# One value block per pair of heads in an attention and mixture-of-experts kernel, with the probabilities of both heads in one tile

## The chip, the core and the metric

The kernel runs on one core of one Trainium2 chip, the other cores idle. The metric is the device time of one execution in microseconds (us). Before the change the median of 3 runs is 830.39 us (829.68 to 831.4).

## What is computed

Causal attention with a bias from accumulated gates for 8 batches of 8 heads, 576 tokens and 64 dimensions per head; then a layer of 8 experts that sends each of the 4608 tokens to one expert and scales its output by the gate. Everything is float32.

```python
scores = scale * np.matmul(q, k.transpose(0, 1, 3, 2))
cum = np.cumsum(np.maximum(s, 0.0), axis=-1)
bias = -(cum[:, :, :, None] - cum[:, :, None, :])
scores = np.where(causal, -1e9, scores + np.minimum(bias, 0.0))
attn = np.exp(scores - np.max(scores, axis=-1, keepdims=True))
attn = attn / (np.sum(attn, axis=-1, keepdims=True) + 1e-09)
x = np.matmul(attn, v)                      # then tokens x 512
e = argmax(x @ w_gate + modality_bias[modality_id])
out = gate * (np.maximum(x @ w1[e], 0.0) @ w2[e])
```

## The kernel before, in words

The first half of the program is attention, the second routing and experts; the change is in the first. Attention goes over 32 **pairs**: one head of two batches (ab = 0, 1) at a time, eight pairs for each of four groups of batches. `run` lays nine steps of each pair out in a row, in the order `ORDER` = 3, 7, 2, 6, 8, 1, 5, 0, 4. Step i below 8 is chunk c = i % 4 of head i // 4: 128 queries against 128(c+1) keys. Step 8 is the last 64 queries of both heads at once, against all 576 keys in two halves of 288.

A **step** is `score`: two matmuls on PE, a high part (L373, KA by QH, called H below) and a low part (L395, KB by QL, called L; for step 8 four of each kind of half length, L408 and L409, h and l), into one of the four PSUM buffers `sp`; a mask and row minimum on DVE (L397, for step 8 L411; R below); an exponential with row sums on ACT (L417, E). Three steps later `trans` follows: PE turns the probabilities 128 by 128 (L427, for step 8 L440; T) into one of two PSUM buffers `pt`, and a copy brings them to the tile PT of the head, on ACT (L430), for step 8 on DVE (four copies, L446).

`tail` runs twice per pair. The **value block** g = 1, for queries 256 to 575, is ten matmuls of the values V by PT (L467), the two heads side by side in halves of the array; it comes two steps after step 8 is turned, when chunks 2 and 3 are in PT as well. Block g = 0, for queries 0 to 255, is four matmuls after the last turn. Each block is copied out of PSUM to oT (ACT L470, and for g = 1 also DVE L474), then multiplied with a small matrix that moves it to tokens by dimensions (`pw`, `pq`, L347, into the one PSUM buffer `ox`; called x below), its row sums are inverted (ACT L479, DVE L480), and DVE multiplies and stores (L489, L491; X below). Every matmul runs as two passes, which the trace shows as two records. `prep` makes the operands of the next pair on POOL (L323, L327), SP moves data with DMAs; `load_v` fetches V of the next pair into one of three buffers.

```python
ORDER = (3, 7, 2, 6, 8, 1, 5, 0, 4)
LAG = 3      # steps from score to trans
TD = 1       # steps from trans to a value block
self.PT = [c.tile([P, PTW], F32, name=f"PT{u}") for u in range(3)]
```

The order in which each engine takes its work comes from a list scheduler that follows the data and the few `issue_after` constraints, so it differs between pairs where other work (routing of a finished group, in the first pairs of the next) lies between. The change reaches `tail`, `trans`, `start`, `score`, `load_v`, `consts` and `run`.

Of the kernel before, what the change touches and what calls it, by code (L numbers as in the profile page):

```python
# [17 lines left out]
P = 128  # L18
KW = 576
# [9 lines left out]
PTDVE = (8,)  # L29
QUIET = (0, 1, 5)  # L30
# [7 lines left out]
class Attn:  # L38
# [3 lines left out]
    def __init__(self, ctx, tc, qkv, s, ident, wg):  # L42
# [14 lines left out]
        self.PT = [c.tile([P, PTW], F32, name=f"PT{u}") for u in range(3)]  # L57
        self.oT = [c.tile([P, 640], F32, name=f"oT{u}") for u in range(2)]
# [10 lines left out]
        sr = t1.tile([P, KW], F32, name="sr")  # L69
# [21 lines left out]
        s8 = t1.tile([P, KW], F32, name="s8")  # L91
# [199 lines left out]
    def consts(self):  # L291
        nc = self.nc
        for u in range(2):
            nc.gpsimd.memset(self.oT[u][:, 512:], 0.0)
        for t in self.PT:
            nc.vector.memset(t[64:, PTW - 64:], 0.0)
# [11 lines left out]
    def load_v(self, pi):  # L308
        V = self.ld.tile([P, 2, 5, 64], F32, name="V", bufs=3)
        self.nc.sync.dma_start(V, self.qkv[pi, :, 4 * KW:].rearrange("p (a j d) -> p a j d", a=2, j=5))  # L310
        return V

# [48 lines left out]
    def start(self, pi, x):  # L361
        st = dict(pi=pi, h=pi % 8, x=x, s={}, high={}, PT=[self.PT[(2 * pi + ab) % 3] for ab in range(2)], V=self.V.pop(pi))
        st["mx"] = self.sm.tile([P, 10], F32, name="mx")
        st["sums"] = self.sm.tile([P, 9], F32, name="sums")
        return st
# [10 lines left out]
    def score(self, st, i):  # L376
# [5 lines left out]
        if i < 8:  # L382
# [4 lines left out]
            t = self.wk.tile([P, 512], F32, name="pe", bufs=6)  # L387
# [31 lines left out]
    def trans(self, st, i):  # L419
        nc = self.nc  # L420
        pe, PT = st["s"].pop(i), st["PT"]
        cp = nc.vector.tensor_copy if i in PTDVE else nc.scalar.copy
        if i < 8:
            ab, c = i // 4, i % 4
            pt = self.ps1.tile([P, 512], F32, name="pt")
            for j in range(c + 1):
                self.pe.append(nc.tensor.transpose(out=pt[:, P * j:P * j + P], in_=pe[:, P * j:P * j + P], identity=self.ident).ins)  # L427
            v = min(P * c, 320)
            w = PT[ab][:, P * c - v:P * c - v + PTS * (c + 1)].rearrange("p (j s) -> p j s", s=PTS)
            cp(w[:, :, v:v + P], pt[:, :P * (c + 1)].rearrange("p (j q) -> p j q", q=P))  # L430
        else:
            for j0, nj in ((0, 4), (4, 1)):
# [8 lines left out]
                for ab in range(2):  # L441
                    if nj == 4:
                        w = PT[ab][:, 128:128 + 4 * PTS].rearrange("p (j s) -> p j s", s=PTS)[:, :, 384:]
                    else:
                        w = PT[ab][:kp, PTW - 64:].unsqueeze(1)
                    cp(w, pt[:kp, :P * nj].rearrange("p (j a q) -> p a j q", a=2, q=64)[:, ab])  # L446

    def tail(self, st, g):
# [3 lines left out]
        for _ in range(TD + g):  # L452
            yield
        q0, q1 = (256, KW) if g else (0, 256)
        o = st["o"] if g else self.ps2.tile([P, 512], F32, name="o")
        oT = self.oT[st["pi"] % 2]

        pe, self.pe = self.pe, []
        nj = 5 if g else 2
        for j in range(nj):  # L460
            f = max(P * j, q0)
            for ab in range(2):
                r = slice(64 * ab, 64 * ab + 64)
                with ExitStack() as after:
                    for i in pe:
                        after.enter_context(self.tc.issue_after(i))
                    m = nc.tensor.matmul(o[r, f - q0:q1 - q0], V[:, ab, j, :], PT[ab][:, PTS * j + f if j < 4 else PTW - 64:PTS * j + q1 if j < 4 else PTW], start=j == 0, stop=j == nj - 1)  # L467
            pe = [m.ins]
        self.wall = m.ins
        nc.scalar.copy(oT[:, q0:q0 + 256], o[:, :256])  # L470
        if g:
            for ab in range(2):
                r = slice(64 * ab, 64 * ab + 64)
                nc.vector.tensor_copy(oT[r, 512 + 64 * ab:576 + 64 * ab], o[r, 256:320])  # L474
        yield
        n = 5 if g else 4
        rs = self.sm.tile([P, 5], F32, name="rs")
        with self.tc.issue_after(self.hold[0]), self.tc.issue_after(self.act):
            nc.scalar.activation(rs[:, :n], st["sums"][:, 4 * g:4 * g + n], AF.Identity, bias=self.eps[:, :1])  # L479
            nc.vector.reciprocal(rs[:, :n], rs[:, :n])  # L480
        xo = self.xo
        for u in range(2):
            c = 2 * g + u
            self.pw_(xo[:, 2 * XW * u:2 * XW * u + 2 * XW], oT[:, P * c:P * c + P], self.pw[:, h, :], start=True, stop=True)
        if g:
            self.pw_(xo[:, 4 * XW:5 * XW], oT[:, 512:], self.pq[:, h, :], start=True, stop=True)
        src = xo[:, :4 * XW].rearrange("p (t d) -> p t d", t=4)
        rv = rs[:, :4].unsqueeze(2).broadcast_to([P, 4, XW])
        nc.vector.tensor_tensor(x[g][:, :, :, h], src.rearrange("p t (d r) -> p t d r", r=2), rv.rearrange("p t (d r) -> p t d r", r=2), ALU.mult)  # L489
        if g:  # L490
            nc.vector.tensor_scalar(x[2][:, 0, :, h], xo[:, 4 * XW:5 * XW].rearrange("p (d r) -> p d r", r=2), rs[:, 4:5], None, ALU.mult)  # L491
# [894 lines left out]
```

## Time and profile before

| | |
|---|---|
| median of 3 runs | 830.39 us |
| profiled execution | 829.02 us, of which the span of recorded instructions is 827.3 us |
| PE busy | 812.1 us (98%) |
| DVE, ACT, POOL busy | 545.6 (66%), 541.3 (65%), 360.5 us (44%) |
| granted TensorE clock, mean | 0.996 of full speed |
| end of attention | about 380 us of the span |

A busy share says how long an engine had some instruction in it, not how fast it went. PE's records overlap (a matmul's record runs on while the next starts), so the distance from one start to the next, in the timeline, tells what a matmul costs; a timeline row gives the start, the time to the end of the last record, the number of records, and in square brackets an idle time and what ended it.

### The profile page before, as it was taken

The numbers are of one execution on the slowest core, as the hardware profiler recorded it, in microseconds if no ns is written. First come the engines' busy times: TensorE is split into PE (matmuls) and PEld (weight loads), VectorE is DVE, ScalarE is ACT, GpSimd is POOL, SyncE is SP. The second block draws the span as 40 slices with busy tenths as digits, with TensorE's granted clock in tenths as the row PEclk, the third lists the DMA queues.
The fourth block names the chain that finished last, engine by engine and source line by source line (L and its number), as shares of the span: only waits on it lengthen the run. The fifth ranks groups of instructions, "written<-read, shape, count | busy, mean of one in ns | idle before, by whom it ended". The sixth has DMA issues, their size and how long they took to land. (4 is left out here: it accounts for less than half of the span.)

```text
span 827.3 us, 16879 instructions
## 1 busy us (share of the span) xinstructions
PE 812.1 (98%) x5692; PEld 695.5 (84%) x5692; DVE 545.6 (66%) x1502; ACT 541.3 (65%) x1292; POOL 360.5 (44%) x384
## 2 busy tenths in 40 slices
PE   7999999999999999999999999999999999999997
PEld 6778877877887878887888899998888999988884
DVE  7666667667666677766489865555666656555874
ACT  6788888888888888885365554444455555444663
POOL 8959768988689867992501000000000000000001
PEclk9999999999999999999999999999999999999999
DMA  7665555866567657738697866655556776555970
GB/s 238 187 195 180 180 179 181 254 223 195 170 182 230 208 155 213 226 97 288 222 381 291 312 259 257 229 202 197 213 201 244 258 258 243 199 202 207 380 247 28
DMA packets 68549, 182.31 MB, mean 220 GB/s; under 512 B 7993, under 2 KB 8889, under 8 KB 68334
## 3 DMA queue, kind: packets, MB, share of 16 engines
q1 hardware_dynamic: 62622, 161.17, 57.5%
q0 software_dynamic: 5840, 20.06, 6.3%
q8 instruction: 45, 0.74, 0.4%
q14 instruction: 42, 0.34, 0.1%
HBM read 144.73 MB, written 26.80 MB: 207 GB/s over the span
## 5 line engine op out<-in xcount | busy, mean ns | idle before, releaser
L1067 POOL DMA_INDIRECT out<-ys,oi x36 | 36.5, 1015 | 368.6 <-ACT ys L1066 297.5
L397 DVE CUSTOM_DVE_ANT_0 pe<-sp,mk 128x512 f32<-128x512 f32 (+3 forms) x256 | 121.2, 487 | 63.2 <-PE sp L395 55.5
L417 ACT ACTIVATE pe<-pe,mx 128x512 f32<-128x512 f32 (+3 forms) x256 | 143.8, 562 | 22.4 <-DVE mx L397 21.0
L427 PE MATMUL pt<-ident,pe 128*128 128x128 f32 x640 | 117.7, 281 | 4.0 <-ACT PT L430 2.8
L430 ACT COPY PT<-pt 128x512 f32<-128x512 f32 (+3 forms) x256 | 106.3, 416 | 13.3 <-PE pt L427 12.6
L1083 ACT ACTIVATE hT<-hp 128x512 fp32r<-128x512 f32 x72 | 42.8, 595 | 93.1 <-PE hp L1081 92.6
L467 PE MATMUL o<-PT,V 128*64 128x320 f32 (+4 forms) x896 | 100.7, 364 | 0.0
L373 PE MATMUL sp<-KA,QH 128*128 128x256 f32 (+2 forms) x256 | 97.3, 389 | 2.5 <-POOL KA L236 2.5
L427 PEld LDWEIGHTS pt<-ident,pe 128*128 128x128 f32 x640 | 75.4, 141 | 26.8 <-ACT PT L430 11.2
L467 PEld LDWEIGHTS o<-PT,V 128*64 128x64 f32 x896 | 58.7, 136 | 41.0 <-issue 9.4
L1081 PE MATMUL hp<-xT,wcb 128*128 128x256 f32 x648 | 89.6, 282 | 0.0
L395 PE MATMUL sp<-KB,QL 76*128 76x256 f32 (+2 forms) x256 | 88.4, 349 | 0.0
L1081 PE MATMUL hp<-xT,wca 128*128 128x256 f32 x624 | 87.3, 282 | 0.5 <-ACT xT L1033 0.5
L327 POOL TENSOR_TENSOR KA<-rawk,KA 64x576 fp32r<-64x576 f32 x62 | 87.0, 1419 | 0.2
L327 POOL TENSOR_TENSOR QL<-rawq,QH 64x576 fp32r<-64x576 f32 x62 | 86.6, 1413 | 0.2
L1084 DVE SCALAR_TENSOR_TENSOR hT<-hp,hT 128x512 fp32r<-128x512 f32 x72 | 49.5, 687 | 55.1 <-ACT hT L1083 54.9
L1081 PEld LDWEIGHTS hp<-xT,wcb 128*128 128x128 f32 x648 | 83.1, 188 | 0.6
L1081 PEld LDWEIGHTS hp<-xT,wca 128*128 128x128 f32 x624 | 80.4, 188 | 1.4 <-issue 0.7
L1056 PE MATMUL y<-wcb,hT 128*128 128x512 f32 x336 | 81.2, 398 | 0.0
L1056 PEld LDWEIGHTS y<-wcb,hT 128*128 128x128 f32 x336 | 62.7, 188 | 14.7
L1081 PE MATMUL hp<-xT,wcc 128*128 128x256 f32 x456 | 64.6, 281 | 0.0
L1056 PE MATMUL y<-wca,hT 128*128 128x512 f32 x264 | 63.9, 398 | 0.0
(285 smaller groups left out, 1611.9 us busy)
## 6 DMA issues: line engine op xcount, KB each, us to landing
wrbw<-in_w SPq DMA_DIRECT2D x104, 512.0 KB
wraw<-in_w SPq DMA_DIRECT2D x56, 512.0 KB
rawq<-in_qkv SPq DMA_DIRECT2D x31, 576.0 KB
rawk<-in_qkv SPq DMA_DIRECT2D x31, 576.0 KB
xg<-lists SPq DMA_DIRECT2D x18, 576.0 KB
V<-in_qkv SPq DMA_DIRECT2D x32, 320.0 KB
KB<-KA SPq DMA_DIRECT2D x62, 144.0 KB
lists<-z SPq DMA_DIRECT2D x8, 576.0 KB
```

Of the source, the lines that this page charges most:

```text
L327: self.last = nc.gpsimd.tensor_tensor(o, i, h, ALU.subtract).ins
L373: self.pe.append(self.nc.tensor.matmul(sp[:, :nn], QH[:, q0:q0 + P], self.KA[u][:, ab, :nn], start=True, stop=False).ins)
L395: self.pe.append(nc.tensor.matmul(sp[:, :nn], QL[:EXT, q0:q0 + P], KB[:EXT, ab, :nn], start=False, stop=True).ins)
L397: ins = nc.vector.tensor_tensor_reduce(out=t[:, :n], in0=sp[:, :n], in1=self.mk[:, 512 - n:512], scale=-0.125, scalar=3.0e38, op0=ALU.add, ...
L417: self.act = nc.scalar.activation(t[:, :n], t[:, :n], AF.Exp, bias=m, scale=-1.0, accum_out=st["sums"][:, o:o + 1]).ins
L427: self.pe.append(nc.tensor.transpose(out=pt[:, P * j:P * j + P], in_=pe[:, P * j:P * j + P], identity=self.ident).ins)
L430: cp(w[:, :, v:v + P], pt[:, :P * (c + 1)].rearrange("p (j q) -> p j q", q=P))
L467: m = nc.tensor.matmul(o[r, f - q0:q1 - q0], V[:, ab, j, :], PT[ab][:, PTS * j + f if j < 4 else PTW - 64:PTS * j + q1 if j < 4 else PTW], ...
L1056: self.last[0] = nc.tensor.matmul(y[u], hT[:, a, f, P * u:P * u + P], W[4 + f // 2][:, c, 512 * (f % 2):512 * (f % 2) + 512], start=f == 0 ...
L1081: nc.tensor.matmul(hp[:, u], W[k][:, a, f:f + P], xT[:, c, k], start=k == 0 and i == 0, stop=k == 3 and i == 2)
L1083: hi = nc.scalar.activation(hs, hp, AF.Relu)
L1084: lo = nc.vector.scalar_tensor_tensor(hT[:, 1, 2 * m:2 * m + 2], hp, 0.0, hs.bitcast(F32), ALU.max, ALU.subtract)
```

## The change

The probabilities of both heads now lie in one tile PT, and there are two of these, for even and odd pairs, in place of three single ones. Chunks 0 and 1 (`JOINT`) are turned for both heads into one `pt` buffer, at the later head's step, and go out with one ACT copy of 256 or 512 columns; step 8 has two DVE copies in place of four. `tail` runs once per pair, after the last turn: one block of 18 matmuls in which every key block j has a matmul of 512, 384, 256 or 128 columns into `o` and one of 64 columns into a further `sp` buffer; one copy of 512 columns to oT on ACT; one inversion of nine sums; then the x matmuls and stores of g = 1 and, one step later, of g = 0. V has two buffers and is loaded at step 5 in place of step 2, oT has one tile, the score tiles `pe` have two buffers for each width in place of six of full width, and two start-up tiles lie inside PT.

```diff
+JOINT = (0, 1)
...
-        self.PT = [c.tile([P, PTW], F32, name=f"PT{u}") for u in range(3)]
-        self.oT = [c.tile([P, 640], F32, name=f"oT{u}") for u in range(2)]
+        self.PT = [c.tile([P, 2, PTW], F32, name=f"PT{u}") for u in range(2)]
+        self.oT = c.tile([P, 640], F32, name="oT")
...
-        sr = t1.tile([P, KW], F32, name="sr")
+        sr, s8 = (self.PT[1][:, 0, KW * u:KW * u + KW] for u in range(2))
...
-        V = self.ld.tile([P, 2, 5, 64], F32, name="V", bufs=3)
+        V = self.ld.tile([P, 2, 5, 64], F32, name="V")
...
-        st = dict(pi=pi, h=pi % 8, x=x, s={}, high={}, PT=[self.PT[(2 * pi + ab) % 3] for ab in range(2)], V=self.V.pop(pi))
+        st = dict(pi=pi, h=pi % 8, x=x, s={}, high={}, PT=self.PT[pi % 2], V=self.V.pop(pi))
...
-            t = self.wk.tile([P, 512], F32, name="pe", bufs=6)
+            t = self.wk.tile([P, n], F32, name=f"pe{c}")
...
-        pe, PT = st["s"].pop(i), st["PT"]
+        PT = st["PT"]
         cp = nc.vector.tensor_copy if i in PTDVE else nc.scalar.copy
+        if i in JOINT:
+            return
         if i < 8:
             ab, c = i // 4, i % 4
+            both = i - 4 in JOINT
             pt = self.ps1.tile([P, 512], F32, name="pt")
-            for j in range(c + 1):
-                self.pe.append(nc.tensor.transpose(out=pt[:, P * j:P * j + P], in_=pe[:, P * j:P * j + P], identity=self.ident).ins)
+            n = P * (c + 1)
+            for a in range(1 - both, 2) if ab else (0,):
+                pe = st["s"].pop(4 * a + c)
+                for j in range(c + 1):
+                    o = n * (a if both else 0) + P * j
+                    self.pe.append(nc.tensor.transpose(out=pt[:, o:o + P], in_=pe[:, P * j:P * j + P], identity=self.ident).ins)
             v = min(P * c, 320)
-            w = PT[ab][:, P * c - v:P * c - v + PTS * (c + 1)].rearrange("p (j s) -> p j s", s=PTS)
-            cp(w[:, :, v:v + P], pt[:, :P * (c + 1)].rearrange("p (j q) -> p j q", q=P))
+            h = slice(0, 2) if both else slice(ab, ab + 1)
+            w = PT[:, h, P * c - v:P * c - v + PTS * (c + 1)].rearrange("p a (j s) -> p a j s", s=PTS)
+            cp(w[:, :, :, v:v + P], pt[:, :n * (1 + both)].rearrange("p (a j q) -> p a j q", a=1 + both, q=P))
         else:
+            pe = st["s"].pop(i)
             for j0, nj in ((0, 4), (4, 1)):
                 if nj == 4:
                     pt = self.ps1.tile([P, 512], F32, name="pt")
                 kp = P if nj == 4 else 64
                 for j in range(nj):
                     self.pe.append(nc.tensor.transpose(out=pt[:kp, P * j:P * j + P], in_=pe[:, P * (j0 + j):P * (j0 + j) + kp], identity=self.ident).ins)
+                if nj == 4:
+                    w = PT[:, :, 128:128 + 4 * PTS].rearrange("p a (j s) -> p a j s", s=PTS)[:, :, :, 384:]
+                    cp(w, pt[:, :512].rearrange("p (j a q) -> p a j q", a=2, q=64))
+                else:
+                    cp(PT[:kp, :, PTW - 64:], pt[:kp, :P].rearrange("p (a q) -> p a q", a=2))
+
+    def tail(self, st):
...
+        o, ox = st["o"], self.ps1.tile([P, 512], F32, name="sp", bufs=SPB)
+        oT = self.oT
+
+        pe, self.pe = self.pe, []
+        for j in range(5):
+            for q0, q1, t, b in ((P * j, 512, o, 0), (512, KW, ox, 512)):
+                if q0 == q1:
+                    continue
                 for ab in range(2):
+                    r = slice(64 * ab, 64 * ab + 64)
+                    with ExitStack() as after:
+                        for i in pe:
+                            after.enter_context(self.tc.issue_after(i))
+                        m = nc.tensor.matmul(t[r, q0 - b:q1 - b], V[:, ab, j, :], PT[:, ab, PTS * j + q0 if j < 4 else PTW - 64:PTS * j + q1 if j < 4 else PTW], start=j == 0, stop=j == (4 if b else 3))
+                pe = [m.ins]
+        self.wall = m.ins
+        nc.scalar.copy(oT[:, :512], o)
+        for ab in range(2):
+            r = slice(64 * ab, 64 * ab + 64)
+            nc.vector.tensor_copy(oT[r, 512 + 64 * ab:576 + 64 * ab], ox[r, :64])
+        yield
+        rs = self.sm.tile([P, 9], F32, name="rs")
+        with self.tc.issue_after(self.hold[0]), self.tc.issue_after(self.act):
+            nc.scalar.activation(rs, st["sums"], AF.Identity, bias=self.eps[:, :1])
+            nc.vector.reciprocal(rs, rs)
+        xo = self.xo
+        for g in (1, 0):
+            for u in range(2):
+                c = 2 * g + u
+                self.pw_(xo[:, 2 * XW * u:2 * XW * u + 2 * XW], oT[:, P * c:P * c + P], self.pw[:, h, :], start=True, stop=True)
+            if g:
+                self.pw_(xo[:, 4 * XW:5 * XW], oT[:, 512:], self.pq[:, h, :], start=True, stop=True)
+            src = xo[:, :4 * XW].rearrange("p (t d) -> p t d", t=4)
+            rv = rs[:, 4 * g:4 * g + 4].unsqueeze(2).broadcast_to([P, 4, XW])
+            nc.vector.tensor_tensor(x[g][:, :, :, h], src.rearrange("p t (d r) -> p t d r", r=2), rv.rearrange("p t (d r) -> p t d r", r=2), ALU.mult)
+            if g:
+                nc.vector.tensor_scalar(x[2][:, 0, :, h], xo[:, 4 * XW:5 * XW].rearrange("p (d r) -> p d r", r=2), rs[:, 8:9], None, ALU.mult)
             yield
...
-                if k % 9 == 2 and 0 < pi < npair - 1:
+                if k % 9 == 5 and 0 < pi < npair - 1:
                     self.V[pi + 1] = self.load_v(pi + 1)
...
-                _, st, g = prev.pop(0)
-                if g == 0 and st["pi"] % 8 == 7:
+                _, st = prev.pop(0)
+                if st["pi"] % 8 == 7:
...
-                if i0 in (8, ORDER[-1]):
-                    g = int(i0 == 8)
-                    prev.append((self.tail(sts[p0], g), sts[p0], g))
+                if i0 == ORDER[-1]:
+                    prev.append((self.tail(sts[p0]), sts[p0]))
```

In a pair in the middle (most pairs look alike) the rows of three engines stand as follows; `PT_109` to `PT_111` are the PT tiles, `sp`, `o`, `pt` and `ox` are PSUM buffers.

PE before, from the last part of step 8 over value block g = 0 to the x matmuls after it; block g = 1 (ten rows of L467) comes 21 rows further on.

```order
L409 MATMUL sp<-KB_108,QL_104 128x288
L467 MATMUL o<-PT_111,V 64x256
L467 MATMUL o<-PT_109,V 64x256
L467 MATMUL o<-PT_111,V 64x128
L467 MATMUL o<-PT_109,V 64x128
L427 MATMUL pt<-ident,pe 128x128 x4
L373 MATMUL sp<-KA_106,QH_102 128x256
L395 MATMUL sp<-KB_108,QL_104 128x256
L347 MATMUL ox<-pw,oT_112 128x144 x2
L427 MATMUL pt<-ident,pe 128x128 x3
```

PE now, at the same place; no further value block follows until the next pair's.

```order
L474 MATMUL o<-PT_110,V 64x512 x2
L474 MATMUL sp<-PT_110,V 64x64 x2
L474 MATMUL o<-PT_110,V 64x384 x2
L474 MATMUL o<-PT_110,V 64x256 x2
L474 MATMUL o<-PT_110,V 64x128 x2
L474 MATMUL sp<-PT_110,V 64x64 x4
L433 MATMUL pt<-ident,pe_2277 128x128 x4
L372 MATMUL sp<-KA_105,QH_101 128x256
L394 MATMUL sp<-KB_107,QL_103 128x256
L346 MATMUL ox<-pw,oT 128x144 x2
L346 MATMUL ox<-pq,oT 128x72
```

The two blocks became one, with 64-column matmuls between the wide ones, and the first x matmuls are now those of g = 1.

DVE before, from the store X of g = 0 over the copies of step 8 to the first reductions of the next pair (128 columns are step 4 of the old pair, 512 step 3 of the new; `mx` alone is the read of a row minimum).

```order
L489 TENSOR_TENSOR x<-ox,rs 128x144x2
L446 COPY PT_110<-o 64x64
L446 COPY PT_110<-pt 128x4x64
L446 COPY PT_111<-pt 128x4x64
L446 COPY PT_111<-o 64x64
L397 ISA pe,mx<-sp,mk 128x128
L397 ISA mx 128x1
L397 ISA pe,mx<-sp,mk 128x512
```

DVE now, at the same place.

```order
L495 TENSOR_TENSOR x<-ox,rs 128x144x2
L497 TENSOR_SCALAR xq<-ox,rs 128x36x2
L451 COPY PT_109<-pt 128x2x4x64
L453 COPY PT_109<-o 64x2x64
L495 TENSOR_TENSOR x<-ox,rs 128x144x2
L396 ISA pe_2409,mx<-sp,mk 128x128
L396 ISA mx 128x1
L396 ISA pe_2417,mx<-sp,mk 128x512
```

The store of g = 0 stands behind the copies of step 8 now, immediately ahead of the reductions; on PE its x matmuls stand behind both parts of the first 512-column score of the new pair.

ACT before, from the exponentials of the new pair's steps 3 and 7 over the copies of chunk 0 of the old one.

```order
L417 ACTIVATE pe,sums<-pe,mx 128x512 x2
L470 COPY oT_113<-o 128x256
L430 COPY PT_110<-pt 128x128
L430 COPY PT_111<-pt 128x128
L417 ACTIVATE pe,sums<-pe,mx 128x384
L479 ACTIVATE rs<-sums,eps 128x5
L430 COPY PT_109<-pt 128x4x128
```

ACT now, at the same place.

```order
L437 COPY PT_109<-pt 128x2x2x128
L416 ACTIVATE pe_2409,sums<-pe_2409,mx 128x128
L416 ACTIVATE pe_2417,sums<-pe_2417,mx 128x512
L416 ACTIVATE pe_2435,sums<-pe_2435,mx 128x512
L416 ACTIVATE pe_2443,sums<-pe_2443,mx 128x384
L437 COPY PT_109<-pt 128x2x128
L416 ACTIVATE pe_2454,sums<-pe_2454,mx 128x384
```

The last copy that the old pair's value block needs (two heads of 128 columns) now stands behind three exponentials of the new pair, steps 3, 7 and 2. It stands so in 14 of the 31 pairs that have a successor; in 3 it is behind the first two, in 8 behind the first alone, in 6 ahead of all.

## Rows read from the trace of the kernel before

**Rows 1.** Windows, 100 to 200 and 400 to 800 us: busy us per engine, clock, DMA, GB/s.

```profile
100.00:200.00 100.00, 99.69 (x785) 80.40 (x784) 68.41 (x296) 83.42 (x274) 82.68 (x81) 1.00 0.64 201
400.00:800.00 400.00, 400.00 (x2582) 362.66 (x2582) 255.59 (x347) 206.74 (x260) 38.92 (x39) 1.00 0.69 252
```

**Rows 2.** Timeline of PE, one quiet pair: start, us to the last end, records, [idle before].

```profile
187.82 0.30 PE L409 MATMUL sp<-KB,QL 76*128 76x288 f32 x1
188.05 0.87 PE L467 MATMUL o<-PT,V 128*64 128x256 f32 x8
188.85 0.65 PE L427 MATMUL pt<-ident,pe 128*128 128x128 f32 x4
...
192.16 0.48 PE L395 MATMUL sp<-KB,QL 76*128 76x512 f32 x1
192.47 0.40 PE L373 MATMUL sp<-KA,QH 128*128 128x512 f32 x1
192.72 0.38 PE L427 MATMUL pt<-ident,pe 128*128 128x128 f32 x2
192.85 0.47 PE L395 MATMUL sp<-KB,QL 76*128 76x512 f32 x1
193.34 0.41 PE L427 MATMUL pt<-ident,pe 128*128 128x128 f32 x2
193.69 2.28 PE L467 MATMUL o<-PT,V 128*64 128x320 f32 x20
195.89 0.33 PE L427 MATMUL pt<-ident,pe 128*128 128x128 f32 x1
195.97 0.42 PE L373 MATMUL sp<-KA,QH 128*128 128x384 f32 x1
196.23 0.34 PE L395 MATMUL sp<-KB,QL 76*128 76x384 f32 x1
196.41 0.27 PE L427 MATMUL pt<-ident,pe 128*128 128x128 f32 x1
...
197.60 0.60 PE L427 MATMUL pt<-ident,pe 128*128 128x128 f32 x4
...
199.21 0.44 PE L467 MATMUL o<-PT,V 128*64 128x256 f32 x2
```

**Rows 3.** Timeline of DVE in the same pair: a store, a copy, two reductions.

```profile
191.84 0.46 DVE L489 TENSOR_TENSOR x<-ox,rs 128x288 f32<-128x288 f32 x1
192.21 0.20 DVE L446 COPY PT<-o 64x64 f32<-64x64 f32 x1
...
193.11 0.28 DVE L397 CUSTOM_DVE_ANT_0 pe<-sp,mk 128x128 f32<-128x128 f32 x1
...
193.32 0.69 DVE L397 CUSTOM_DVE_ANT_0 pe<-sp,mk 128x512 f32<-128x512 f32 x1
```

**Rows 4.** Timeline of ACT in the same pair: two exponentials.

```profile
194.15 0.72 ACT L417 ACTIVATE pe<-pe,mx 128x512 f32<-128x512 f32 x1
...
197.56 0.62 ACT L417 ACTIVATE pe<-pe,mx 128x384 f32<-128x384 f32 x1 [0.58 <-DVE mx L397]
```

**Rows 5.** Lines of ACT by form, 100 to 420 us: busy us, mean ns, idle before.

```profile
L470 ACT COPY oT<-o 128x256 f32<-128x256 f32 x50 | 18.6, 372 | 23.8 <-PE o L467 23.4
L430 ACT COPY PT<-pt 128x256 f32<-128x256 f32 x50 | 18.2, 364 | 6.1 <-PE pt L427 5.9
L430 ACT COPY PT<-pt 128x128 f32<-128x128 f32 x50 | 13.3, 269 | 4.2 <-PE pt L427 4.2
```

**Rows 6.** Timeline of PE: block g = 0 four pairs after the end of Rows 2.

```profile
244.59 0.65 PE L467 MATMUL o<-PT,V 128*64 128x256 f32 x4
```

**Rows 7.** Timeline of PE at the end of attention.

```profile
377.62 0.87 PE L467 MATMUL o<-PT,V 128*64 128x256 f32 x8
378.99 0.76 PE L347 MATMUL ox<-pw,oT 128*128 128x144 f32 x4 [0.50 <-ACT oT L470]
379.58 1.04 PE L1031 MATMUL tp<-ident,xg 128*128 128x128 f32 x8
```

More of the change, by code (lines that the diff above doesn't have):

```diff
@@ L90, in __init__ @@
         self.warm(WARM)
-        s8 = t1.tile([P, KW], F32, name="s8")
         for k in HALVES:
@@ L292, in consts @@
         nc = self.nc
-        for u in range(2):
-            nc.gpsimd.memset(self.oT[u][:, 512:], 0.0)
+        nc.gpsimd.memset(self.oT[:, 512:], 0.0)
         for t in self.PT:
-            nc.vector.memset(t[64:, PTW - 64:], 0.0)
+            nc.vector.memset(t[64:, :, PTW - 64:], 0.0)
     def raws(self):
@@ L440, in trans @@
                     self.pe.append(nc.tensor.transpose(out=pt[:kp, P * j:P * j + P], in_=pe[:, P * (j0 + j):P * (j0 + j) + kp], identity=self.ident).ins)
[L441 to L446, printed above, removed]
@@ L448, in tail @@
-    def tail(self, st, g):
+                if nj == 4:
[4 more added lines that the diff above has]
+    def tail(self, st):
         nc = self.nc
         V, PT, x, h = st["V"], st["PT"], st["x"], st["h"]
-        for _ in range(TD + g):
+        for _ in range(TD):
@@ L453, in tail @@
             yield
-        q0, q1 = (256, KW) if g else (0, 256)
-        o = st["o"] if g else self.ps2.tile([P, 512], F32, name="o")
-        oT = self.oT[st["pi"] % 2]
+        o, ox = st["o"], self.ps1.tile([P, 512], F32, name="sp", bufs=SPB)
+        oT = self.oT
         pe, self.pe = self.pe, []
[L459 to L468, printed above, removed]
@@ L469, in tail @@
-        self.wall = m.ins
[L470 to L474, printed above, removed]
+        for j in range(5):
[9 more added lines that the diff above has]
+                pe = [m.ins]
@@ L475, in tail @@
+        self.wall = m.ins
+        nc.scalar.copy(oT[:, :512], o)
+        for ab in range(2):
+            r = slice(64 * ab, 64 * ab + 64)
+            nc.vector.tensor_copy(oT[r, 512 + 64 * ab:576 + 64 * ab], ox[r, :64])
         yield
-        n = 5 if g else 4
-        rs = self.sm.tile([P, 5], F32, name="rs")
+        rs = self.sm.tile([P, 9], F32, name="rs")
         with self.tc.issue_after(self.hold[0]), self.tc.issue_after(self.act):
-            nc.scalar.activation(rs[:, :n], st["sums"][:, 4 * g:4 * g + n], AF.Identity, bias=self.eps[:, :1])
-            nc.vector.reciprocal(rs[:, :n], rs[:, :n])
+            nc.scalar.activation(rs, st["sums"], AF.Identity, bias=self.eps[:, :1])
+            nc.vector.reciprocal(rs, rs)
@@ L481, in tail @@
         xo = self.xo
[L482 to L489, printed above, removed]
@@ L490, in tail @@
-        if g:
-            nc.vector.tensor_scalar(x[2][:, 0, :, h], xo[:, 4 * XW:5 * XW].rearrange("p (d r) -> p d r", r=2), rs[:, 4:5], None, ALU.mult)
+        for g in (1, 0):
[10 more added lines that the diff above has]
+            yield
```

## The prediction

> **What bounds the kernel now.** I read the windows first: between 100 and 200 us PE is busy 99.69 of 100 us at full granted clock, DVE 68, ACT 83, POOL 83, and from 400 to 800 us PE has no idle time at all [rows 1]. So PE's order of work sets the end, and a microsecond won or lost in attention is carried to the last instruction unchanged. Next the timeline of PE through one quiet pair [rows 2], from one block g = 0 (188.05) to the next (199.21): 11.16 us. The reader is to look at the distances of starts. After L of 512 columns at 192.16 the next matmul starts 0.31 later; after the same L at 192.85 the transposes start 0.49 later. So PE waits there, some 0.18 us, for a copy to empty `pt`. It is the one wait of a quiet pair. Then the timelines of DVE and ACT in the same pair [rows 3, 4], for what one reduction, store or exponential takes from start to next start. A wait of either engine costs nothing until PE waits for it.
>
> **The change, part by part.**
>
> *One value block for two.* The columns stay: g = 1 streams 1216 columns per head in one pass and g = 0 streams 384, the new block 1280 and 320. With two passes at 1.2 columns per ns for the two heads side by side the old blocks need 2.03 and 0.64 us; start to next transpose they take 2.20 and 0.80 [rows 2], so each has about 0.16 us beyond its columns. Into a block it is 0.23 us (187.82 to 188.05), where the eight matmuls of step 8 stand about 0.14 apart. One block less saves 0.16 + 0.09 = 0.25 us per pair. The new block should take 2.67 + 0.16 = 2.8 us.
>
> *The narrower matmuls.* There are 36 records per pair for 28. The two old blocks differ by 12 records and by 1.40 us, of which their columns are 1.39 [rows 2]: a record costs about 1 ns beyond its columns, the eight added ones nothing. The Trainium skill (TensorEngine Tiling (Array Packing), Instruction Overhead) says otherwise, that a matmul of one column takes as long as one of 60, through an overhead of some 60 cycles; eight more at 25 ns would by that estimate add 0.2 us per pair, 6 us in all. The trace does not bear that out, and the sum goes by the rows.
>
> *Copies and sums.* ACT has 0.27 us for one copy of 128 columns and 0.36 for one of 256 [rows 5]; the joint copy of chunk 0 so takes between 0.36 (same columns) and 0.54 (two copies). I take 0.36, as the copies' time follows their columns. One copy of chunk 1, one copy to oT, one inversion and two small copies on DVE go too. All this lies beside PE's work, on engines with a sixth or more of their time idle [rows 1], and is worth nothing by itself. It would be worth something only where PE waits for it, which is the next part. The DVE copies to oT no longer share a PSUM buffer with ACT's; their wait was off PE's path as well.
>
> *What is now late.* The x matmuls of g = 0 moved behind the first 512-column score of the new pair, and on DVE their store X stands ahead of the reductions of steps 4, 3, 7 and 2. On ACT the exponentials of 3, 7 and 2 stand ahead of the joint copy of chunk 0, and the whole value block now waits for that copy. Before, its g = 0 part alone did, half a pair later. I walk both engines from the first transpose after these x matmuls, time 0. The last x record ends about 0.16 later (0.17 between the starts and ends at 378.99 and 379.58 [rows 7]), X starts at 0.20. Then in this order: X 0.37, reduction of 128 columns 0.21, of 512 columns to its end 0.69 [rows 3], 0.10 to ACT, two exponentials of 512 at 0.72 and one of 384 at 0.62 [rows 4], the copy 0.36 [rows 5], 0.05 to PE: 4.04 us. The allowances between engines are bounded by nothing and the 0.13 left of the wait of 0.50 less the copy's 0.37 [rows 5, 7]. PE itself needs from the same point [rows 2]: four transposes 0.35 (0.11 apart), H and L of 512 columns 0.56 (192.16 to 192.72), H and L of 384 0.44 (195.97 to 196.41), then T, H, T, L 0.63 (0.08 + 0.26 + 0.11 + 0.18), and four transposes with step 8 up to the value block 1.61 (197.60 to 199.21): 3.59 us. So the value block waits 0.45 us. The reductions of 2 and 6 finish in time behind this and are not waited for.
>
> *Two small waits.* The same walk makes the transposes of step 8 wait 0.17 for `pt`, which ACT empties after a copy of 512 columns, an exponential of 256 and the inversion, and those of step 4 wait 0.05. The old wait of 0.18 before step 5's transposes goes: they share a buffer with step 1's.
>
> *A quiet pair* thus changes by -0.25 - 0.18 + 0.45 + 0.22 = **+0.24 us**. There are 13 of them (4 to 7, 12 to 15, 20 to 23 and 30): +3.1 us.
>
> *Pairs beside a routing.* In the twelve such pairs the printed order sets the joint copy ahead of all, one or two of those exponentials. From 199.21 to 244.59 [rows 2, 6] four such pairs take 45.38 us; the same walk along their new order gives 11.39, 10.76, 11.47 and 10.81, together 44.43. That is -0.95 per group, -2.8 for three. Pairs 28 and 29, with the copy behind one exponential, give -0.4 each. The bounds are -0.43 per pair (no wait, no new small wait) and +0.24 (as in the quiet ones).
>
> *Begin and end.* Pairs 1 to 3 have half an order of each kind and low halves that wait for DMAs; I take +0.3 together, between -1.3 and +1.5. In the last pair nothing covers the tail: x of g = 0 must wait until X of g = 1 has left `ox`, and the copy to oT is one of 512 columns. Before, from block g = 0 to the next phase's first transposes it was 1.96 us (377.62 to 379.58 [rows 7]) with 0.50 idle; I add the second wait, 0.4 to 1.2, and take +0.8.
>
> *V, DMAs, POOL.* V goes two buffers deep and its DMA, three steps later, waits for the value block of the pair before last. On SP nothing changes place but this, the loads behind it are for the pair after next, and V has over a pair to land. I cost it at nothing; if that cover failed the value block would be late by the landing.
>
> *Sum:* 3.1 - 2.8 - 0.8 + 0.3 + 0.8 = **+0.6 us** on the profiled 829.0, so 829.6. The median of the runs is 1.4 above the profiled execution; the forecast is 830.4 + 0.6 = **831.0 us**. An error of 0.1 us in the walk of a pair is 3 us in the sum, and its likely own range is 826 to 836.
>
> **The rivals.**
>
> *A, the copy comes in time.* If DVE or ACT get through their queues 0.45 us faster than walked, only the block saved and the old wait removed are left. For it: in 17 of 31 pairs the copy is not behind all three exponentials, and both engines idle. Against it: each step of the walk is a strict order with rows of its own. Price: 31 x (-0.25 - 0.18 + 0.22) + 0.8 = -5.7, so 824.7; without the small waits too 31 x -0.43 + 0.8 = -12.5, so 817.9.
>
> *B, the wait is in every pair.* ACT's copy of chunk 0 holds the value block in all 31 pairs as in the quiet ones: 31 x 0.24 + 0.8 = +8.2, so 838.6. If the joint copy takes 0.54 too, 844. It decides from the point where the new waits pass 0.43 us in the mean pair, the small ones included. For it: PE is 98% busy and has no other work in this stretch that may pass the block, since the following transposes are held behind it. Against it: the printed order of 17 pairs.
>
> *C, narrow matmuls cost more than their columns.* If each of the eight added records cost as much as a whole 64-column record does at 1.2 columns per ns side by side, 0.027 us, the block would be 0.21 longer and the time 31 x 0.21 = 6.6 higher, 837.6. The 12 records that cost 0.01 together [rows 2] speak against it; the page named above speaks for it.
>
> **How the numbers follow.** My case has 0.50, A 0.26, B 0.20, C 0.04. A measurement of this kernel can tell about 0.2% from no change, 1.7 us. Within my case, faster than 828.7 takes a fifth, between the bounds two fifths, slower two fifths. Faster: 0.26 + 0.10 = 0.36; same 0.20; slower 0.20 + 0.04 + 0.20 = 0.44. The range goes from 820, inside A's two prices, to 840, just past B's, and leaves out A's far end and B's worst.
>
> **What would show it.** In the changed profile, a quiet pair of 11.3 to 11.5 us from value block to value block, one block of about 2.8 us, and idle time of PE (or of its weight loads) before it, put down to ACT's copy to PT. The pairs beside a routing should lie near 11 us. The wait before step 5's transposes should be gone. The idle time of DVE before X of g = 0 should grow, and that before the copies to oT should no longer name ACT. The prediction fails if quiet pairs come at 11.0 or less (A), if all pairs are longer than 11.3 (B), if the block takes 3.0 (C), or if the second half, from the first expert on, changes its length.

## The result and the profile after

The changed kernel takes 833.5 us (median of 6 runs, 832.93 to 834.97), the kernel before 829.77 us (6 runs, 829.05 to 831.4): a ratio of 1.0046, 95% interval 1.0034 to 1.0057. It is slower by 3.7 us, in the forecast range (820 to 840), on the side that had the largest chance, and six times as much as the +0.6 us of the sum. The span of the profiled execution grew from 827.3 to 831.3 us.

The windows of the kernel after (columns as in [rows 1]):

```profile
100.00:200.00 100.00, 98.00 (x859) 81.20 (x857) 63.61 (x270) 78.28 (x238) 84.00 (x83) 1.00 0.66 207
400.00:800.00 400.00, 400.00 (x2582) 362.71 (x2581) 255.66 (x347) 206.11 (x260) 40.90 (x41) 1.00 0.69 252
```

DVE and ACT have some 5 us less to do in 100, copies and inversions; PE, which sets the end, now has 2.0 us of idle time in the first window where it had 0.3. The second half keeps its length up to 808 us (see the end of this section).

The timeline of PE in a quiet pair of the kernel after, answering to [rows 2]:

```profile
176.76 1.08 PE L474 MATMUL o<-PT,V 128*64 128x512 f32 x4 [0.30 <-ACT PT L437]
...
179.32 0.40 PE L474 MATMUL sp<-PT,V 128*64 128x64 f32 x8
179.65 0.66 PE L433 MATMUL pt<-ident,pe 128*128 128x128 f32 x4
...
183.63 0.65 PE L346 MATMUL ox<-pw,oT 128*128 128x144 f32 x4
184.12 0.60 PE L433 MATMUL pt<-ident,pe 128*128 128x128 f32 x4
...
187.51 0.29 PE L408 MATMUL sp<-KB,QL 76*128 76x288 f32 x1
188.12 0.65 PE L474 MATMUL o<-PT,V 128*64 128x512 f32 x2 [0.32 <-ACT PT L437]
```

Value block to value block it is 11.36 us (11.16 before). The block itself takes 2.89 us to the next transposes, its last eight narrow records 0.33 of them (0.21 are columns, the rest the way out of the block). Ahead of it stands the new wait: 0.61 us from the last matmul of step 8, where 0.23 is the distance without a wait, so 0.38 us, put down to ACT's copy to PT. The timeline of DVE in the same pair:

```profile
184.32 0.46 DVE L495 TENSOR_TENSOR x<-ox,rs 128x288 f32<-128x288 f32 x1 [0.26 <-PE ox L346]
184.70 0.28 DVE L396 CUSTOM_DVE_ANT_0 pe<-sp,mk 128x128 f32<-128x128 f32 x1
...
184.90 0.69 DVE L396 CUSTOM_DVE_ANT_0 pe<-sp,mk 128x512 f32<-128x512 f32 x1
```

And that of ACT:

```profile
184.76 0.59 ACT L437 COPY PT<-pt 128x512 f32<-128x512 f32 x1 [1.23 <-PE pt L433]
185.24 0.40 ACT L416 ACTIVATE pe<-pe,mx 128x128 f32<-128x128 f32 x1
...
185.69 0.73 ACT L416 ACTIVATE pe<-pe,mx 128x512 f32<-128x512 f32 x1
...
186.41 0.71 ACT L416 ACTIVATE pe<-pe,mx 128x512 f32<-128x512 f32 x1
...
187.12 0.60 ACT L416 ACTIVATE pe<-pe,mx 128x384 f32<-128x384 f32 x1
...
187.72 0.35 ACT L437 COPY PT<-pt 128x256 f32<-128x256 f32 x1
```

This is the predicted chain: the store 0.20 after the transposes, the reduction of step 3 done at 185.59, its exponential 0.10 later, three exponentials, the copy, and the value block 4.00 us after the transposes (4.04 walked). One thing the prediction did not see: ACT's own queue, from the joint copy of chunk 1 (184.76) and the exponential of step 4, comes free at about 185.64, within 0.05 us of the reduction. The chain has two heads. By the distances of starts, the two small waits of the walk come to about 0.12 us each (0.17 and 0.05 walked).

Three more places cost time. First the early pairs. The timeline of SP in the kernel after, at V's first load in the loop:

```profile
30.25 0.33 SPq L309 DMA_DIRECT2D V<-in_qkv  x1
30.63 0.42 SPq L304 DMA_DIRECT2D rawq<-in_qkv  x1
31.11 0.42 SPq L304 DMA_DIRECT2D rawk<-in_qkv  x1
```

POOL there, at the preparation that uses these loads:

```profile
37.46 1.30 POOL L322 TENSOR_SCALAR KA<-rawk 128x576 fp32r<-128x576 f32 x2 [4.20 <-PE sp L408]
```

PE there, two pairs on:

```profile
58.53 0.50 PE L372 MATMUL sp<-KA,QH 128*128 128x512 f32 x1 [0.44 <-POOL KA L326]
...
59.90 0.86 PE L372 MATMUL sp<-KA,QH 128*128 128x512 f32 x3 [0.64 <-POOL KA L326]
```

The same instructions of SP in the kernel before:

```profile
26.24 0.57 SPq L310 DMA_DIRECT2D V<-in_qkv  x1
26.87 0.44 SPq L305 DMA_DIRECT2D rawq<-in_qkv  x1
27.35 0.44 SPq L305 DMA_DIRECT2D rawk<-in_qkv  x1
```

And of POOL in the kernel before:

```profile
33.87 1.31 POOL L323 TENSOR_SCALAR KA<-rawk 128x576 fp32r<-128x576 f32 x2 [0.45 <-DMA rawk<-in_qkv]
```

V's DMA goes out 4.0 us later (the first value block, 27.25 to about 30.2 us, still reads its buffer), the loads of k and q behind it 3.8 us later, POOL's preparation 3.6 us later, 6.4 to 6.5 us after the load in both; later still PE waits for POOL. The wait named at POOL's row is that of the last semaphore by the profile; by these distances it was the DMA. The last score of pair 4 begins at 70.14 in place of 67.75, **2.4 us late**, of which 0.1 was there from the start.

Second, in pair 30 PE waits once for a DMA of the next pair's low rows (and the pair takes 11.98 us):

```profile
364.38 0.50 PE L394 MATMUL sp<-KB,QL 76*128 76x512 f32 x1 [0.44 <-DMA KB<-KA]
```

Third, the end of attention, answering to [rows 7]:

```profile
376.90 1.08 PE L474 MATMUL o<-PT,V 128*64 128x512 f32 x4 [0.46 <-ACT PT L437]
...
380.31 0.76 PE L346 MATMUL ox<-pw,oT 128*128 128x144 f32 x4 [0.45 <-ACT oT L477]
...
381.99 0.76 PE L346 MATMUL ox<-pw,oT 128*128 128x144 f32 x4 [0.75 <-DVE xq L497]
382.58 1.04 PE L1037 MATMUL tp<-ident,xg 128*128 128x128 f32 x8
```

The first transposes of the experts come at 382.58, 3.00 us after the 379.58 of before, and PE's matmuls stay 3.00 to 3.01 late up to 808 us. Between the two last scores and these transposes 0.9 of it arose. The other 1.0 of the span appears in the last 20 us; in the versions below that stretch differs by 0.0 to 0.8 us, so I do not put it down to the change.

### The profile page after: what moved, and what is told of

It is laid out like the page before. It is cut to its first block, busy times and chain, and to the rows that moved or that the text cites. A ratio compares the mean times of both kernels' runs of the same rounds, so it can differ in the third digit from the quotient of the medians.

```text
span 831.3 us, 17195 instructions
## 1 busy us (share of the span) xinstructions
PE 807.9 (97%) x5948; PEld 696.2 (84%) x5948; DVE 526.3 (63%) x1405; ACT 524.6 (63%) x1164; POOL 360.8 (43%) x383
## 5 line engine op out<-in xcount | busy, mean ns | idle before, releaser
L416 ACT ACTIVATE pe<-pe,mx 128x512 f32<-128x512 f32 (+3 forms) x256 | 142.6, 559 | 12.1 <-DVE mx L396 11.5
L396 DVE CUSTOM_DVE_ANT_0 pe<-sp,mk 128x512 f32<-128x512 f32 (+3 forms) x256 | 117.8, 485 | 48.2 <-PE sp L394 22.7
L437 ACT COPY PT<-pt 128x512 f32<-128x512 f32 (+1 forms) x192 | 94.1, 505 | 41.8 <-PE pt L433 41.7
L433 PE MATMUL pt<-ident,pe 128*128 128x128 f32 x640 | 109.2, 277 | 3.6 <-ACT pe L416 2.9
L474 PE MATMUL o<-PT,V 128*64 128x256 f32 (+3 forms) x512 | 87.2, 440 | 4.4 <-ACT PT L437 4.3
L394 PE MATMUL sp<-KB,QL 76*128 76x256 f32 (+2 forms) x256 | 84.4, 337 | 0.5 <-DMA KB<-KA 0.4
L474 PEld LDWEIGHTS sp<-PT,V 128*64 128x64 f32 x640 | 39.4, 137 | 34.4 <-issue 22.0
L322 POOL TENSOR_SCALAR KA<-rawk 128x576 fp32r<-128x576 f32 x60 | 39.8, 672 | 58.8 <-PE sp L372 35.3
```

The lines of the kernel that those rows point to most:

```text
L394: self.pe.append(nc.tensor.matmul(sp[:, :nn], QL[:EXT, q0:q0 + P], KB[:EXT, ab, :nn], start=False, stop=True).ins)
L396: ins = nc.vector.tensor_tensor_reduce(out=t[:, :n], in0=sp[:, :n], in1=self.mk[:, 512 - n:512], scale=-0.125, scalar=3.0e38, op0=ALU.add, ...
L416: self.act = nc.scalar.activation(t[:, :n], t[:, :n], AF.Exp, bias=m, scale=-1.0, accum_out=st["sums"][:, o:o + 1]).ins
L433: self.pe.append(nc.tensor.transpose(out=pt[:, o:o + P], in_=pe[:, P * j:P * j + P], identity=self.ident).ins)
L437: cp(w[:, :, :, v:v + P], pt[:, :n * (1 + both)].rearrange("p (a j q) -> p a j q", a=1 + both, q=P))
L474: m = nc.tensor.matmul(t[r, q0 - b:q1 - b], V[:, ab, j, :], PT[:, ab, PTS * j + q0 if j < 4 else PTW - 64:PTS * j + q1 if j < 4 else PTW], ...
```

## The experiments

"Late at pair 4" below is the begin of the last score of pair 4 against 67.75 us before (the change has +2.4). It holds what was late at the last score of pair 0 already (21.00 us before): 0.0 to 0.4 in most runs, but -0.6 in run 5, +0.6 in run 9, +1.2 in run 7 and +1.4 in run 11. Up to there all versions of the changed kernel have the same order on every engine, so this is the start of one execution and not the edit. One thing that differs there is the granted clock of TensorE, which has two levels in these rows, 0.5 and 1.00 of full speed (0.66 is a mean of both); the windows of run 11 and of run 8:

```profile
16.00:21.00 5.00, 4.75 (x22) 4.13 (x22) 3.19 (x12) 3.84 (x10) 4.92 (x7) 0.66 0.94 291
16.00:21.00 5.00, 4.27 (x29) 3.46 (x30) 3.80 (x17) 5.00 (x15) 4.92 (x7) 1.00 0.91 280
```

In run 8 the stretch at the lower clock comes earlier (0.66 between 11 and 16 us, where run 11 has 1.00). Each comparison of times is with the kernel before, run on the same chip.

**1. V behind the loads of q and k.** `k % 9 == 5` becomes `k % 9 == 8` at V's load.

> The changed kernel with one edit: V of the next pair is loaded at step 8, behind the loads of q and k, in place of step 5, ahead of them. My account of the early pairs: with two buffers V's DMA waits for a value block (issued at 30.25 us where before it was issued at 26.24), and the loads of q and k, the gate rows and then POOL's preparation stand behind it on SP. Then pairs 1 to 4, which lost 2.3 us against before (last score of pair 4 at +2.40), should lose at most 0.5, pair 30's extra 0.6 may go too, and the time falls by 1.8 to 2.5 us from 833.5 to 831.0 to 831.7. Quiet pairs stay at 11.36. Rival: the early pairs are long because of the printed order of the score halves; then the time stays at 833.5 and the last score of pair 4 at +2.4.

832.42 us, ratio 1.0033 (1.0021 to 1.0044). Late at pair 4: 1.38 us; experts' first transposes 2.2 us late in place of 3.0. So V's place on SP is about 1.0 of the early 2.3 us, not all of it: pair 3 goes from 13.35 to 12.31 us from value block to value block (11.82 before), and PE no longer waits for POOL there. The rival, the printed order, may hold for the rest; this run does not show it. Most quiet pairs 11.36.

**2. V's part alone in the kernel before.** `bufs=3` goes, `k % 9 == 2` becomes `== 5`.

> The kernel before with the change's V part alone: two buffers, loaded at step 5. By the account that V's wait holds SP, the early pairs lose here what they lost in the change, 1.5 to 2.4 us, with quiet pairs at 11.16 as before: 831.3 to 832.2 against 829.8. By the rival, that the V part is hidden and the value block's order made the early pairs long, it stays within 0.4 of 829.8.

837.68 us, ratio 1.0081 (1.0061 to 1.0102), three to four times what I expected. Late at pair 3: 2.0 us, at pair 4 7.9, at the end of attention 9.6; most quiet pairs are as before. The row of the worst wait, in PE's timeline:

```profile
61.46 0.80 PE L373 MATMUL sp<-KA,QH 128*128 128x512 f32 x1 [3.09 <-POOL KA L327]
```

So V's part is not hidden; alone it costs more than the whole change. The lateness adds up: POOL's two preparations start at 38.54 and 54.73 where before they started at 33.87 and 47.23, 4.7 and 7.5 us late. And of the 5.9 us that pair 4 alone loses, 3.1 are the wait above; with the other 2.8 goes the granted clock, which fell to the lower level at the end of that wait, as the window shows (in the kernel before it was 1.00 there):

```profile
61.02:67.85 6.83, 5.92 (x20) 3.50 (x22) 2.27 (x8) 2.52 (x8) 2.69 (x4) 0.50 0.58 222
```

Value block g = 1, which lies there, takes 3.10 us to the next transposes (2.20 before). Of the four executions the one with a mean granted clock of 0.997 took 835.04 us, the others, with 0.992 or 0.993, 837.29 to 838.8. What else makes V's part dearer here than by run 1 in the change was not tried.

**3. The copy ahead.** The exponential of step 2 is created after the joint copy of chunk 0.

```diff
+        if i == 2 and st["pi"] > 0:
+            self.late = lambda: nc.scalar.activation(t[:, :n], t[:, :n], AF.Exp, bias=m, scale=-1.0, accum_out=st["sums"][:, o:o + 1]).ins
+            return
...
+                if i0 == ORDER[-1] and self.late is not None:
+                    with self.behind(), self.tc.issue_after(self.copy0):
+                        self.act = self.late()
```

> The changed kernel with one edit to ACT's order: the exponential of step 2 of the next pair is issued behind the joint copy of chunk 0 in place of ahead of it. DVE's and PE's orders stay, the store of g = 0 is still ahead of the reductions. The value block of a quiet pair waits 0.38 us for this copy; the copy comes 0.6 us earlier. If this wait is what the quiet pairs lost, they fall from 11.36 to 10.98, 0.38 in each of 14, and the time falls by 4.5 to 5.5 us to 828.0 to 829.0. Rival 1: another wait stands right behind it (the exponential of step 2 then holds the transposes, or a score buffer), then quiet pairs fall by less than 0.2 and the time by less than 3. Rival 2: the block waits for the store on DVE and not for the copy's place; then nothing changes.

830.32 us, ratio 1.0006 (0.9994 to 1.0018). Seven of the 13 quiet pairs fall to 10.96 to 10.99, as expected, without the wait ahead of the block; the others take up to 11.5. But late at pair 4: 3.7 us. A row of its PE timeline and one of POOL's show where it went:

```profile
59.30 0.51 PE L373 MATMUL sp<-KA,QH 128*128 128x512 f32 x1 [1.12 <-POOL KA L327]
...
52.55 1.31 POOL L323 TENSOR_SCALAR KA<-rawk 128x576 fp32r<-128x576 f32 x2 [5.64 <-PE sp L409]
```

PE waits for a preparation that POOL starts at 52.55, 0.8 us later than in the change (51.79). What makes it later was not tried.

**4. The store later, the copy still late.** Four more `yield` between x of g = 1 and of g = 0; the joint copy of chunk 0 held behind the exponential of step 2.

> The changed kernel with the x matmuls and the store of g = 0 four steps later (behind the reductions of steps 4, 3 and 7), and the joint copy of chunk 0 held behind the exponentials of steps 3, 7 and 2 in all pairs, as it is in the quiet pairs of the change. My prediction's chain began with that store at the head of DVE's queue: if it is the cause, R of step 3 ends 0.6 or more earlier, and the wait of 0.38 us goes: quiet pairs near 11.0. Rival: ACT's own queue from the joint copy of chunk 1 on (copy 0.48, exponentials 0.45, 0.72, 0.72, 0.60, copy 0.35) sets the end; on PE the transposes for that copy come 0.49 earlier here, so the wait would go as well, but in after.py's order they stood behind the x matmuls; then R of step 3 is ready long before its exponential starts, which the timeline tells. Because the copy is late in all pairs, the twelve pairs beside a routing should not be faster than the quiet ones.

830.11 us, ratio 1.0000 (0.9988 to 1.0012): most quiet pairs 10.81, late at pair 4 3.8 us, the pairs beside a routing 10.8 to 11.7. So with the copy behind all three exponentials the wait also goes. ACT in such a pair:

```profile
95.56 0.58 ACT L440 COPY PT<-pt 128x512 f32<-128x512 f32 x1 [0.74 <-PE pt L435]
96.05 0.41 ACT L416 ACTIVATE pe<-pe,mx 128x128 f32<-128x128 f32 x1
...
96.44 0.71 ACT L416 ACTIVATE pe<-pe,mx 128x512 f32<-128x512 f32 x1
...
98.46 0.35 ACT L440 COPY PT<-pt 128x256 f32<-128x256 f32 x1
```

ACT runs without a gap from the copy of chunk 1; the reduction of step 3 was done at 96.16, 0.28 before its exponential. Moving the x matmuls moved both heads of the chain at once, the store on DVE and the transposes of chunk 1 on PE. With ACT alone as its head the exponential of step 3 starts 0.39 us after that of step 4 (96.05 to 96.44); in the change it was 0.45 (185.24 to 185.69). By these rows the store held the chain there by 0.06 us only, and moving the store without the transposes could have won no more; that was not tried.

**5. V loaded in its own pair.**

```diff
...
-                if k % 9 == 5 and 0 < pi < npair - 1:
-                    self.V[pi + 1] = self.load_v(pi + 1)
+                if k % 9 == 3 and pi > 1:
+                    sts[pi]["V"] = self.load_v(pi)
```

> The changed kernel with one edit: V of a pair is loaded at step 3 of the pair itself (it is read a pair later), so that its buffer has been free for half a pair when its DMA comes up on SP and nothing stands behind a waiting DMA. If V's wait on SP is what the early pairs lost, the last score of pair 4 comes at +0.6 or less against before, where the change had +2.40 and the load at step 8 had +1.38, and the time falls by 1.8 to 2.4 us to 831.1 to 831.7. If something else makes these pairs long (the printed order of the score halves, the gate rows), it stays at or above the 832.4 of the load at step 8. Quiet pairs stay at 11.36.

832.82 us, ratio 1.0033 (1.0021 to 1.0046). Late at pair 4: 1.3 us, about as in run 1, though this run was 0.6 ahead at pair 0; pair 3 takes 12.32, as in run 1. So over 1 us of the early loss is not V's. Pair 30 is a quiet pair again (11.36), and at the last score the kernel is only 0.2 us late, where the change is 2.1. It comes back in the last value block, as V of the last pair now stands behind two loads of weights on SP; the two rows are of PE's timeline, the third of the windows:

```profile
374.19 0.33 PE L433 MATMUL pt<-ident,pe 128*128 128x128 f32 x1 [1.06 <-ACT pe L416]
375.69 1.93 PE L474 MATMUL o<-PT,V 128*64 128x512 f32 x4 [1.17 <-DMA V<-in_qkv]
```

```profile
375.69:378.80 3.11, 3.11 (x12) 1.33 (x14) 0.00 (x0) 0.00 (x0) 2.10 (x1) 0.51 1.04 375
```

The block begins 1.2 us ahead of the change's and ends 0.5 behind it: the lower clock took 1.7 us of what was won.

**6. Without the joint copies.** `JOINT = ()`.

> The changed kernel without the joint copies: chunks 0 and 1 are turned and copied head by head again, four copies on ACT in place of two, 0.34 us more of ACT's time per pair. The printed order then has the last copy of chunk 0 behind two exponentials, not three. If the wait of the value block is a matter of the place of that copy, it goes, the quiet pairs fall to about 11.0 although ACT has more to do, and the time falls by 3 to 5 us. If ACT's total work sets the wait, the quiet pairs grow to 11.5 or more.

832.56 us, ratio 1.0037 (1.0027 to 1.0047). Quiet pairs 11.2, late at pair 4 4.3. The expectation had the copy's place wrong. On ACT the last copy of chunk 0 stands behind the same three exponentials as in the change, not two:

```profile
186.80 0.72 ACT L416 ACTIVATE pe<-pe,mx 128x512 f32<-128x512 f32 x1
...
187.53 0.71 ACT L416 ACTIVATE pe<-pe,mx 128x512 f32<-128x512 f32 x1
...
188.23 0.60 ACT L416 ACTIVATE pe<-pe,mx 128x384 f32<-128x384 f32 x1
...
188.83 0.24 ACT L437 COPY PT<-pt 128x128 f32<-128x128 f32 x1
```

PE starts the value block at 188.69 with the first head, whose chunk 0 was copied ahead of these exponentials. So the run does not answer its question; it shows that the quiet pairs do not grow when ACT has 0.34 us more to do.

**7. Both repairs**, runs 3 and 5 together.

> Both repairs together: V loaded in its own pair, and the exponential of step 2 behind the joint copy of chunk 0. Quiet pairs 10.98, early pairs at most +0.8 against before: 833.5 less 2 for V and less 5 for the copy, 826.5 to 828.0, faster than both kernels. With the copy ahead alone the early pairs lost 3.7 us, so that V's part is worth more here; if the early pairs are bound by POOL's preparation instead, they lose 2 or more again and the time is 829 or more.

828.11 us, ratio 0.9978 (0.9967 to 0.9989), faster than both kernels by a little. Late at pair 4: 2.0, of which 1.2 at pair 0, so the early pairs lost 0.9, about as expected; quiet pairs 10.97 to 11.00. The last value block waits 1.44 us for V, and its first four records take 1.97 us, as in run 5 (1.93; the change 1.08).

**8. V in its own pair, and x and store of g = 0 four steps later.**

```diff
             if g:
...
+                for _ in range(4):
+                    yield
             yield
```

> V loaded in its own pair, and x and store of g = 0 four steps later, with nothing forced on ACT: the printed order has the joint copy of chunk 0 behind two exponentials or one. Quiet pairs 10.8, as with the late copy (10.81), the pairs beside a routing 11.0 in the mean, early pairs at most +0.8: 824.5 to 826.5. Rival: with the store behind the reductions the quiet pairs do not fall below 10.95, as with the copy's place alone, and the time is 827 to 828.

**819.71 us, ratio 0.9876 (0.9862 to 0.9890)**: better than expected, the fastest version. Late at pair 4: -0.25; most quiet pairs 10.81, the pairs beside a routing 10.8 to 11.2. PE has no idle time left in the first window:

```profile
100.00:200.00 100.00, 100.00 (x882) 83.91 (x882) 65.42 (x279) 80.89 (x245) 84.84 (x85) 1.00 0.64 208
```

**9. The same without V's repair.**

> The changed kernel with x and store of g = 0 four steps later, and V's load left at step 5 with two buffers: the pair of the 819.7 us kernel without its V repair. If V's wait on SP is worth the more the faster PE runs through the first pairs (1.1 us with the change's order, 1.7 with the copy ahead), the last score of pair 4 comes 3 us or more later than there (+2.8 or more against before, where it was -0.25) and the time is 822.5 to 824. If the order alone had set the early pairs, the time is within 1 us of 819.7.

827.23 us, ratio 0.9966 (0.9952 to 0.9980): late at pair 4: 4.5. Leaving V's load where the change has it costs 7.5 us here; with the change's order it cost 0.7 in all (run 5), and 1.9 up to the last score, of which 0.7 was there at pair 0. The forecast had the mechanism and about half of its size.

**10. Run 8 without the joint copies.**

> The 819.7 us kernel without the joint copies: four copies of chunks 0 and 1 per pair on ACT in place of two. Theory: the joint copies save ACT 0.34 us per pair, and where PE waits for nothing that is worth nothing: quiet pairs stay at 10.8, the time within 1.5 us of 819.7. Rival: ACT has become the chain (in a quiet pair of the late-copy kernel it ran from the copy of chunk 1 to the copy of chunk 0 without a gap), then 0.34 us more of it lengthen the pairs, up to 31 x 0.34 = 10 us, to 830.

829.34 us, ratio 0.9993 (0.9979 to 1.0006): 9.6 us lost. My theory fell, and the rival came near the number: ACT is in the chain. Quiet pairs are 11.02, 0.21 longer and not 0.34; 1.6 us more are lost by pair 4. The line of the list of waits (total, times, longest) that grew, from 2.1 us in run 8:

```profile
PEld pt L433 <- ACT pe L416: 8.5, 26, 1.1
```

The edit also turns the earlier head's chunks at its own step again, so ACT's time and this order are not told apart.

**11. Three steps in place of four.**

> As the 819.7 us kernel, but x and store of g = 0 three steps later, not four: the store stands behind the reductions of steps 4 and 3 and ahead of that of step 7, the joint copy of chunk 0 behind one exponential. If only the copy's place matters, it is as fast, 819 to 821. If the store ahead of the reduction of step 7 delays its exponential and with it the pair, quiet pairs are 10.9 or more and the time 822 or more.

821.91 us, ratio 0.9898 (0.9881 to 0.9914). Quiet pairs 10.79, so in them the store ahead of the reduction of step 7 delays nothing. The loss against run 8 is 2.3 us by pair 4 (2.1 late, where run 8 had -0.25) and the same at the experts' transposes. But 1.3 of it was there at pair 0; in pairs 2 and 3 PE waits once each for an exponential, where run 8 does not:

```profile
48.16 0.33 PE L433 MATMUL pt<-ident,pe 128*128 128x128 f32 x1 [0.37 <-ACT pe L416]
...
60.21 0.33 PE L433 MATMUL pt<-ident,pe 128*128 128x128 f32 x1 [0.37 <-ACT pe L416]
```

So about 1 us is the edit's by these rows. The intervals of the two ratios overlap (run 8: 0.9862 to 0.9890).

## Why the prediction was right, and what it missed

- *What bounds the kernel*: right. The 3.0 us of attention are carried to 808 us unchanged. The signs of failing that the prediction named did not come: quiet pairs above 11.0, not all pairs above 11.3, a block below 3.0, and a second half of the same length up to 808 us.
- *A quiet pair*, +0.24: measured +0.20. The wait ahead of the block was walked as 0.45 and is 0.38. The value block is 2.89 where 2.8 was said, so one block less saves 0.20 and not 0.25. Runs 3 and 4 take the wait away and find 10.98 and 10.81 in most quiet pairs. The walk began at the store on DVE alone; that ACT's own queue leads to the same time within 0.06 us is luck.
- *Narrow matmuls*: nearly right. The block takes 2.89 us for 2.67 of columns, 0.06 more beyond them than the old ones; if all of that were the eight added records, it is 8 ns each. The prediction's estimate of 25 ns each, from the 60 cycles of the Trainium skill (TensorEngine Tiling (Array Packing), Instruction Overhead), does not show in this trace either. That section of the Trainium skill also says that a matmul of one column takes as long as one of 60; read so, as a least time, it asks nothing more of records of 64 columns, and the trace agrees. (Two records per matmul hold for the value and the x matmuls; a score half or a transpose has one in the rows.)
- *Pairs beside a routing*: right in the sum, with luck in it. Four of them took 45.38 us [rows 2, 6]. The two rows that answer, from PE's timeline after, are 44.45 us apart (44.43 walked). The single pairs take 11.65, 10.80, 11.19 and 10.81 where 11.39, 10.76, 11.47 and 10.81 were walked, so two errors of 0.3 cancel:

```profile
199.47 0.65 PE L474 MATMUL o<-PT,V 128*64 128x512 f32 x2 [0.32 <-ACT PT L437]
...
243.92 0.65 PE L474 MATMUL o<-PT,V 128*64 128x512 f32 x2
```

- *Pairs 28 and 29*: -0.8 was said, -0.7 measured. *The last pair*: +0.8 was said, +0.9 measured.
- **What failed is "V, DMAs, POOL ... I cost it at nothing"**, and with it "Pairs 1 to 3 ... I take +0.3 together, between -1.3 and +1.5", which came to +2.3, outside its bounds. The sentence "the loads behind it are for the pair after next" was true and no cover: POOL starts on them as soon as they land. I had checked that V lands in time, and not what stood behind its wait on SP. Of the 2.3 us, about 1.0 is V's place by run 1. The rest goes when the x matmuls of g = 0 move as well (run 8), so it belongs to the change's printed order by that run; which row of it was not tried. Pair 30 (+0.8, where +0.24 was counted) goes with V's place in run 5.
- The terms so come to +2.4 - 2.8 - 0.7 + 2.3 + 0.8 + 0.9 = +2.9, with 0.1 at the start the 3.0 us seen at the experts; the medians say 3.7. Without the early pairs and what pair 30 has beyond a quiet one (2.3 and 0.6) the walked terms come to 0.0, no change: that the time fell on the slower side, clear of the noise, is not the walk's merit.
- *Copies and sums* "worth nothing by itself" held for the change only while another wait hid it. With the waits gone (runs 8 and 10) the joint copies, and the order that goes with them, are worth 9.6 us: ACT's idle share said nothing of ACT's queue between two waits of PE.

## What to carry to other kernels

A load into a buffer that something still reads was a wait on SP here (V's DMA, 4.0 us later than before, and the loads behind it 3.8), and such a wait is to be costed by the work behind it there, down to who starts on that work when it lands, even where the load itself has a pair to spare. When one engine is dense and the others are in order, walk the queue of each from the last thing that it waited for; the busy share does not show a chain that runs without gaps between two waits. A change that is slower by a little can hold a large gain: here four `yield` and the place of one load turned +0.5% into -1.2%.

## What I had not expected of the hardware

- The same wait on SP cost about 1 us in the change's early pairs (runs 1 and 5), 7.5 in all under an order in which PE runs faster (run 9), and some 7 in the kernel before (run 2; 9.6 in its profiled execution, 2.8 of them with the lower clock). In these runs it has no price of its own, only one against what PE does meanwhile.
- In run 5 PE stood idle 1.06 and 1.17 us ahead of the last value block, and the granted clock of the next 3.1 us was 0.51 of full speed, about the lower of its two levels (1.2 of 2.4 GHz); its first four records took 1.93 us where they take 1.08 in the change. In the change, with gaps of 1.07 and 0.46 us at the same place, the clock stayed at 1.00. In runs 5 and 2 a wait of PE so cost more than its length: 1.7 us more in run 5, and some 2.8 more behind the wait of 3.09 us in run 2.
